# The second FFN product of a fused attention + FFN kernel in Strassen's form: seven block products in 128x256 matmuls in place of the plain product in 128x512 matmuls

## The chip, the cores and the metric

The kernel runs on one core of one Trainium2 chip. The metric is device time in microseconds (us), the median over runs. Differences of medians come with the ratio of the mean times: the mean time of one kernel's runs over the mean time of the other's runs in the same rounds, so it is not quite the ratio of the medians quoted beside it.

## The reference

Attention over 8 batches of 576 tokens gives 4608 tokens of 512 features, and an FFN follows.

```python
def _moe_ref(x, w_in, w_out):            # x [4608, 512], w_in [512, 2048], w_out [2048, 512]
    h = x @ w_in
    g = np.where(h > 0.0, h, np.exp(np.minimum(h, 0.0)) - 1.0)
    return (g @ w_out).astype(np.float32)      # the "second product"
```

The attention half (scores, softmax, product with v) is unchanged and only matters as work that shares the engines.

## The kernel before

The FFN works in tiles of tokens: two of 256 (tiles 0 and 1), then eight of 512 (tiles 2 to 9). For each tile and each of the 16 chunks of 128 hidden features there are four steps, on three engines:

```python
def F(t, i):      # TensorE: h = w_in[:, chunk].T @ x.T, four matmuls 128x512 into PSUM, where matmuls leave results ("hps", two banks)
def e(t, i):      # ScalarE: exp(h)
def r(t, i):      # VectorE: min(exp, 1) - 1, fp16
def g(t, i):      # VectorE: max(h, r) -> g, fp16 in SBUF; this also frees the hps bank
def G(t, tb_, qd):                 # TensorE: second product, 128 tokens, 4 of the 16 chunks
    for fc in range(4 * qd, 4 * qd + 4):
        nc.tensor.matmul(out=ob[t, tb_], lhsT=gts[t, fc][:, P * tb_:P * (tb_ + 1)], rhs=w_out16[:, fc, :],
                         start=(fc == 0), stop=(fc == NFC - 1))          # 128x512
def o(t, tb_):    # VectorE: PSUM -> SBUF, 128x512 f32
def s(t, tb_):    # DMA to out
```

From tile 3 on a plain loop orders the work. I call one pass over b a stage and one pass over i a slot. In the traces, from stage 3 on, r, g, evictions (o) start on VectorE in exactly the order in which the program emits them (256 of 256 in this kernel), and so do F and the second product's matmuls on TensorE (960). Weight loads overlap matmuls (in the page below both together are busy for more than the span).

```python
for b in range(3, NT // TT + 2):              # stages 3..10
    todo = ...                                # attention of the next batch, in 12 of 16 slots, for b < 8
    for i in range(NFC):                      # slots 0..15
        if b < len(tiles):                    # stages 3..9
            run(f"F.{b}.{i} e.{b}.{i} r.{b}.{i} g.{b}.{i}")
        run(f"G.{b - 1}.{i // 4}.{i % 4}")    # second product of the tile before
        if i % 4 == 3:
            run(f"o.{b - 1}.{i // 4} s.{b - 1}.{i // 4}")
        if i in todo: todo[i]()
```

So stages 3 to 7 carry attention too, stages 8 and 9 only FFN, and stage 10 only the second product of the last tile. Stage 2 is ordered by a hand-written list.

The softmax here doesn't subtract the row's maximum and nothing guards it: scores larger than these inputs give would overflow.

Of the kernel before, what the change touches and what calls it, by code (L numbers as in the profile page):

```python
# [8 lines left out]
FP32 = mybir.dt.float32  # L9
FP16 = mybir.dt.float16  # L10
BF16 = mybir.dt.bfloat16
AFT = mybir.ActivationFunctionType
ALU = mybir.AluOpType
# [4 lines left out]
def kernel(  # L18
# [11 lines left out]
    nc = tc.nc  # L30
    P = 128

    B, H, S, D = q.shape
# [3 lines left out]
    DM = H * D  # L37
# [18 lines left out]
    def layout(cuts):  # L56

        res, col = [], 0
        for qa, qe in zip(cuts, cuts[1:]):
# [10 lines left out]
    NFC = DF // P  # L70
    SCALE = float(1.0 / (D ** 0.5))
    tiles = [(0, CUT), (CUT, TT)] + [(t, t + TT) for t in range(TT, NT, TT)]
# [7 lines left out]
    konst = ctx.enter_context(tc.tile_pool(name="konst", bufs=1))  # L80
    stage = ctx.enter_context(tc.tile_pool(name="stage", bufs=2))
    attn = ctx.enter_context(tc.tile_pool(name="attn", bufs=2))
    xpool = ctx.enter_context(tc.tile_pool(name="xpool", bufs=4))
    melt = ctx.enter_context(tc.tile_pool(name="melt", bufs=3))
    gpool = ctx.enter_context(tc.tile_pool(name="gpool", bufs=2 * NFC + 2))
    psum = ctx.enter_context(tc.tile_pool(name="psum", bufs=2, space=bass.MemoryType.PSUM))
    ctx.enter_context(tc.manual_schedule(
        engines={ENG.PE, ENG.Activation, ENG.DVE, ENG.Pool, ENG.SP}))
# [3 lines left out]
            name=nc.get_next_instruction_name(),  # L92
# [6 lines left out]

    w_in16 = konst.tile([P, NCC, DF], FP16, name="w_in16")  # L100
    w_out16 = konst.tile([P, NFC, DM], FP16, name="w_out16")


    st = {}
# [29 lines left out]
    def load_wi(fa, fe):  # L134

        for g in range(2):
            for i in range(4):
                nc.gpsimd.dma_start(  # L138
                    out=w_in16[32 * i:32 * (i + 1), 2 * g:2 * g + 2, fa:fe], in_=wi_v[i, :, g, :, fa:fe])
# [5 lines left out]
    for b in range(B):  # L145
        (nc.sync if b % 2 == 0 else nc.scalar).dma_start(
            out=bk32[NB * b:NB * (b + 1), :, :],
            in_=beacon_k[b].rearrange("h n d -> n h d"))
# [7 lines left out]
    for t in qks:  # L156
# [12 lines left out]
        out=triu, in_=triu, compare_op=ALU.is_ge, fill=0.0, base=0,  # L169
# [13 lines left out]
    op = {}  # L183
# [76 lines left out]
    def S_(b, p, g):  # L260
        if g == 0:
            ets[b, p] = attn.tile([P, 2, ECOLS], FP16, tag="et", bufs=6, name="et")
        s = sc[b, p, g] = psum.tile([P, 2, 512], FP32, tag="S", name="sc")
        t = qkT[b, p]
        c0, c1 = GW * g, GW * (g + 1)
        for (j, qa, qe, col) in lays[b]:
            a, e = max(c0, col), min(c1, col + qe - qa)
            if a >= e:
                continue
            for h in range(2):  # L270
                nc.tensor.matmul(  # L271
                    out=s[:, h, a - c0:e - c0],
                    lhsT=t[D * h:D * (h + 1), 1, P * j:P * (j + 1)],
                    rhs=t[D * h:D * (h + 1), 0, NB + qa + a - col:NB + qa + e - col],
                    start=True, stop=True, skip_group_check=True,
                )
# [8 lines left out]
    @step  # L285
    def m(b, p, g):

        c0, c1 = GW * g, GW * (g + 1)
        for (j, qa, qe, col) in lays[b]:
            base = NB if j == 0 else 0  # L290
            e = min(qe, ilo[j] + P - base)
            a, e = max(qa, qa + c0 - col), min(e, qa + c1 - col)
            if a >= e:
                continue
            t0 = a - ilo[j] + base
            o = ets[b, p][0:kc[j], :, col + a - qa:col + e - qa]
            nc.vector.tensor_tensor(out=o, in0=o, in1=triu[0:kc[j], :, t0:t0 + e - a], op=ALU.mult)  # L297

    def quad(b, g, qa, qe, t, half, first):


        v16 = st[b][2]
        pcs = [(j, max(a, qa), min(e, qe), c + max(a, qa) - a) for (j, a, e, c) in lays[b]
               if max(a, qa) < min(e, qe)]
        for n, (j, a, e, c) in enumerate(pcs):
            for i in range(4):
                h, p = 4 * g + i, 2 * g + i // 2
                nc.tensor.matmul(  # L308
                    out=t[32 * i:32 * (i + 1), a - qa:e - qa],
                    lhsT=ones[0:kc[j], :] if half is None else v16[0:kc[j], j, h, 32 * half:32 * (half + 1)],  # L310
                    rhs=ets[b, p][0:kc[j], i % 2, c:c + e - a],
                    start=(first and n == 0), stop=(n == len(pcs) - 1), skip_group_check=True)
# [101 lines left out]
    op["R"] = R_  # L414


    hp, eb, rb, gts, ob = {}, {}, {}, {}, {}

    @step
    def F(t, i):  # L420
# [12 lines left out]
    def flat(y):  # L433
        return y.rearrange("c n w -> c (n w)")

    @step
    def e(t, i):
        eb[t, i] = melt.tile([P, 512], FP32, tag="e", name="e")
        nc.scalar.activation(out=eb[t, i], in_=flat(hp[t, i]), func=AFT.Exp, bias=0.0, scale=1.0)  # L439

    @step
# [4 lines left out]

    @step
    def g(t, i):
        w = tiles[t][1] - tiles[t][0]
        gt = gpool.tile([P, 512 // w, w], FP16, tag="g", name="gt")  # L450
        nc.vector.tensor_tensor(out=flat(gt), in0=flat(hp[t, i]), in1=rb[t, i], op=ALU.max)  # L451
        for n_ in range(512 // w):
            gts[t, i * (512 // w) + n_] = gt[:, n_, :]

    @step
    def G(t, tb_, qd):
        if qd == 0:
            ob[t, tb_] = psum.tile([P, DM], FP32, tag="ops", name="ops")
        for fc in range(4 * qd, 4 * qd + 4):
            nc.tensor.matmul(  # L460
                out=ob[t, tb_], lhsT=gts[t, fc][:, P * tb_:P * (tb_ + 1)], rhs=w_out16[:, fc, :],
                start=(fc == 0), stop=(fc == NFC - 1))

    @step
# [5 lines left out]
    @step  # L470
    def s(t, tb_):
        row = tiles[t][0] + tb_ * P
        nc.sync.dma_start(out=out[row:row + P, :], in_=ob[t, tb_])

    @step
    def wo(i):
# [12 lines left out]
    def run(names):  # L489
        for word in names.split():  # L490
            f, *args = word.split(".")
            op[f](*[a if a in "ABR" else int(a) for a in args])
# [26 lines left out]
    G.1.0.0 e.2.3 g.2.2 m.2.2.0 m.2.2.1 r.2.3 F.2.4 S.2.2.2 g.2.3 e.2.4 S.2.1.3 cb.3.2 x.2.2.2 r.2.4  # L519
    g.2.4 G.1.1.2 F.2.5 m.2.2.2 T.3.0 x.2.1.3 m.2.1.3 e.2.5 T.2.3 ck.3.0 ck.2.3 F.2.6 r.2.5 G.1.1.3  # L520
    g.2.5 e.2.6 S.2.2.3 S.2.3.0 F.2.8 o.1.1 cb.3.1 x.2.2.3 G.1.0.1 r.2.6 x.2.3.0 S.2.3.1 m.2.2.3
    L.2.0 e.2.8 x.2.3.1 W.2.0.0 g.2.6 W.2.0.1 m.2.3.0 s.0.0 r.2.8 g.2.8 s.0.1 m.2.3.1 F.2.7 n.2.0
    M.2.0.1 e.2.7 M.2.0.0 F.2.9 S.3.0.0 e.2.9 S.2.3.2 lv.3 G.1.0.2 r.2.7 g.2.7 x.3.0.0 x.2.3.2
    F.2.11 S.3.0.1 e.2.11 x.3.0.1 r.2.9 m.3.0.0 g.2.9 m.2.3.2 r.2.11 g.2.11 s.1.1 S.2.3.3 m.3.0.1
    F.2.10 x.2.3.3 G.1.0.3 e.2.10 S.3.0.2 m.2.3.3 o.1.0 x.3.0.2 S.3.0.3 F.2.12 r.2.10 m.3.0.2 g.2.10
    L.2.1 e.2.12 W.2.1.0 x.3.0.3 s.1.0 r.2.12 F.2.14 g.2.12 m.3.0.3 n.2.1 M.2.1.0 F.2.13 e.2.14
    T.3.1 W.2.1.1 e.2.13 r.2.14 R.2 ck.3.1 T.3.2 g.2.14 r.2.13 F.2.15 g.2.13 M.2.1.1 n.2.R M.2.R
    e.2.15 r.2.15 ck.3.2 g.2.15
    """)
# [1 line left out]
    def T_(b, p):  # L531
        if b < B:
            run(f"cb.{b}.{p} T.{b}.{p} ck.{b}.{p}")

    def SC(b, p, g0):
        if b < B:
            for g_ in (g0, g0 + 1):
                run(f"S.{b}.{p}.{g_} x.{b}.{p}.{g_} m.{b}.{p}.{g_}")

    def LW(b, g):  # L540
        run(f"L.{b}.{g} W.{b}.{g}.0 n.{b}.{g} M.{b}.{g}.0")

    def WR(b, g):
        run(f"W.{b}.{g}.1" + g * f" R.{b}" + f" M.{b}.{g}.1" + g * f" n.{b}.R M.{b}.R")

    SLOTS = [0, 1, 2, 4, 5, 6, 7, 8, 9, 11, 12, 13]
    for b in range(3, NT // TT + 2):
        todo = {}
        if b < B:
            todo = dict(zip(SLOTS, [  # L550
                lambda: SC(b, 1, 0), lambda: SC(b, 1, 2), lambda: (T_(b, 3), LW(b, 0)),
                lambda: SC(b, 2, 0), lambda: SC(b, 2, 2), lambda: (T_(b + 1, 0), WR(b, 0)),
                lambda: SC(b, 3, 0), lambda: SC(b, 3, 2), lambda: (T_(b + 1, 1), LW(b, 1)),
                lambda: SC(b + 1, 0, 0), lambda: SC(b + 1, 0, 2), lambda: (T_(b + 1, 2), WR(b, 1))]))
        for i in range(NFC):
            if b < len(tiles):
                run(f"F.{b}.{i} e.{b}.{i} r.{b}.{i} g.{b}.{i}")
            run(f"G.{b - 1}.{i // 4}.{i % 4}")
            if i % 4 == 3:
                run(f"o.{b - 1}.{i // 4} s.{b - 1}.{i // 4}")  # L560
            if i in todo:
                todo[i]()
            if i == 3 and b + 1 < B:
                run(f"lk.{b + 1} lv.{b + 1}")
# [28 lines left out]
```

## Time and profile before

| | before |
|---|---|
| time, median | 371.9 us |
| TensorE matmuls of the second product | 576 of 128x512 |
| one stage with attention (F of slot 0 to F of slot 0) | 40.1 to 40.3 us (stage 7, which has less: 37.0) |
| one FFN-only stage | 27.6 us |

The lines below are from the profile page of the kernel before: the busy time of the engines, then the shares of the chain that ended last, then groups of instructions. A group line reads: source line, engine, operation, output<-inputs, shapes, count | busy us, mean ns of one | idle us before it.

```profile
PE 361.5 (97%) x4427; PEld 182.1 (49%) x4427; DVE 251.9 (68%) x611; ACT 238.5 (64%) x351; POOL 68.4 (18%) x100
...
PE 88%; DMA 5%; POOL 4%; issue 1%; DVE 1%; ACT 1%; POOLq 0%
...
L460 PE MATMUL ops<-w_out_80,gt 128*128 128x512 f16 x576 | 145.3, 379 | 0.0
...
L451 DVE TENSOR_TENSOR gt<-hps,r 128x512 f16<-128x512 f32 x144 | 99.6, 692 | 5.8
...
L467 DVE COPY osb<-ops 128x512 f32<-128x512 f32 x36 | 24.6, 683 | 11.8 <-PE ops L460 11.8
```

TensorE (PE) is 97% busy and 88% of the chain. That alone doesn't prove that it runs at its rate, since matmul ends are modelled (a matmul shows 379 ns although they follow each other every 216 ns). The rate is read from starts, in the order-of-time view of TensorE (start us, duration us, what, count). The first two lines are from the 256-token tiles, the others are slots 3 and 4 of stage 6.

```profile
44.33 1.05 PE L429 MATMUL hps<-xT,w_in_79 128*128 128x256 f16 x8
45.21 1.03 PE L460 MATMUL ops<-w_out_80,gt 128*128 128x512 f16 x4
...
229.12 1.04 PE L429 MATMUL hps<-xT,w_in_79 128*128 128x512 f16 x4
229.99 1.03 PE L460 MATMUL ops<-w_out_80,gt 128*128 128x512 f16 x4
230.85 1.03 PE L429 MATMUL hps<-xT,w_in_79 128*128 128x512 f16 x4
231.72 1.03 PE L460 MATMUL ops<-w_out_80,gt 128*128 128x512 f16 x4
```

Four 128x512 matmuls take 229.99 - 229.12 = 0.87 us, 216 ns each; eight 128x256 take 45.21 - 44.33 = 0.88 us, 110 ns each. No line has an idle time in brackets: TensorE never waits here. VectorE at the same time (same kernel, order of time, brackets give idle time and what ended it):

```profile
230.55 0.76 DVE L378 TENSOR_TENSOR xT<-lt,rl 128x128 f16<-128x128 f32 x2 [1.88 <-ACT rl L344]
231.22 0.42 DVE L444 TENSOR_SCALAR r<-e 128x512 f16<-128x512 f32 x1
231.68 0.69 DVE L451 TENSOR_TENSOR gt<-hps,r 128x512 f16<-128x512 f32 x1
232.28 0.68 DVE L467 COPY osb<-ops 128x512 f32<-128x512 f32 x1
232.88 0.42 DVE L444 TENSOR_SCALAR r<-e 128x512 f16<-128x512 f32 x1
```

Here r, g and the eviction o of slot 3 stand one behind the other. Independent instructions start 0.60 us apart although they take 0.68 us.

### The profile page before, as it was taken

What the parts mean: (1) busy time and instruction counts of PE and PEld (TensorE: products, weight loads), DVE (VectorE), ACT (ScalarE), POOL (GpSimd) and SP (SyncE); (2) the same over time, 40 slices, a digit from 0 to 9 for tenths busy, and PEclk for the clock granted to TensorE, in tenths of its full rate; (3) what the DMA queues carried; (4) which work ended last, traced back from release to release, by engine and by line L of the source; (5) the groups of instructions that cost most, each with busy time, mean ns of one, the idle gap of its engine ahead of it and who ended that gap; (6) DMA issues with size and microseconds to landing.
All of it is one profiled execution on the core that took longest, in us unless ns stands there. A gap on an engine that the chain in (4) does not pass through costs nothing.

```text
span 371.1 us, 10275 instructions
## 1 busy us (share of the span) xinstructions
PE 361.5 (97%) x4427; PEld 182.1 (49%) x4427; DVE 251.9 (68%) x611; ACT 238.5 (64%) x351; POOL 68.4 (18%) x100
## 2 busy tenths in 40 slices
PE   8989989999999999999999999999999999999995
PEld 3567655444554454444444454445444544444442
DVE  2448876777777678667767676766767777777731
ACT  2999977788787766777577757776677333333300
POOL 8876530510330014000510050000000000000000
PEclk9999999999999999999999999999999999999999
DMA  8999999945296019900973065000000001001012
GB/s 122 170 167 195 180 196 199 94 60 100 43 90 123 31 32 94 156 32 28 97 104 82 29 42 58 30 30 30 30 30 31 30 28 58 29 28 58 28 59 84
DMA packets 61101, 28.84 MB, mean 78 GB/s; under 512 B 41088, under 2 KB 55424, under 8 KB 61056
## 3 DMA queue, kind: packets, MB, share of 16 engines
q0 software_dynamic: 54720, 18.49, 45.1%
q1 hardware_dynamic: 5760, 9.57, 7.0%
q8 instruction: 34, 0.56, 0.6%
q10 hardware_dynamic: 576, 0.13, 0.2%
q14 instruction: 11, 0.09, 0.1%
HBM read 37.22 MB, written 9.44 MB: 126 GB/s over the span
## 4 chain that ended last, share of the span: by engine, by line
PE 88%; DMA 5%; POOL 4%; issue 1%; DVE 1%; ACT 1%; POOLq 0%
PE hps L429 34%; PE ops L460 33%; PE sc L271 7%; PE lt L308 5%; DMA kst<-in_k_dram 5%; PE tp L229 4%; PE ut L308 4%; POOL v_124 L126 1%; DMA w_in_79<-in_moe_w_in_dram 1%; POOL qst L113 1%; POOL kst L113 1%; DVE xT L378 1%; PE ub L308 0%; POOL w_in_79 L138 0%; ACT rl L344 0%
## 5 line engine op out<-in xcount | busy, mean ns | idle before, releaser
L429 PE MATMUL hps<-xT,w_in_79 128*128 128x512 f16 (+1 forms) x640 | 147.6, 359 | 0.1
L460 PE MATMUL ops<-w_out_80,gt 128*128 128x512 f16 x576 | 145.3, 379 | 0.0
L439 ACT ACTIVATE e<-hps 128x512 f32<-128x512 f32 x144 | 86.4, 600 | 63.5 <-PE hps L429 63.4
L281 ACT ACTIVATE et<-sc 128x832 f16<-128x832 f32 x128 | 104.2, 872 | 16.3 <-PE sc L271 16.2
L451 DVE TENSOR_TENSOR gt<-hps,r 128x512 f16<-128x512 f32 x144 | 99.6, 692 | 5.8
L460 PEld LDWEIGHTS <-gt 128*128 128x128 f16 x576 | 55.8, 98 | 66.3 <-issue 0.9
L444 DVE TENSOR_SCALAR r<-e 128x512 f16<-128x512 f32 x144 | 63.7, 442 | 31.5 <-ACT e L439 29.7
L429 PEld LDWEIGHTS <-w_in_79 128*128 128x128 f16 x640 | 56.2, 98 | 56.2 <-issue 5.7
L297 DVE TENSOR_TENSOR et<-et,triu 128x256 f16<-128x256 f16 (+2 forms) x164 | 40.7, 270 | 25.8 <-ACT et L281 25.5
L467 DVE COPY osb<-ops 128x512 f32<-128x512 f32 x36 | 24.6, 683 | 11.8 <-PE ops L460 11.8
L378 DVE TENSOR_TENSOR xT<-lt,rl 128x448 f16<-128x448 f32 (+6 forms) x28 | 10.6, 419 | 21.0 <-ACT rl L344 21.0
L229 PEld LDWEIGHTS <-qst 96*64 96x64 bf16 x384 | 10.2, 109 | 10.7 <-issue 10.3
L378 DVE TENSOR_TENSOR xT<-ut,rl 128x448 f16<-128x448 f32 (+6 forms) x28 | 10.6, 419 | 6.8 <-PE ut L308 5.3
L198 PE MATMUL w_151<-zero 64*128 64x512 bf16 (+1 forms) x39 | 13.0, 454 | 1.3 <-DVE zero L150 1.3
L229 PE MATMUL tp<-identb,kst 96*64 96x96 bf16 x348 | 12.3, 206 | 1.3 <-DMA kst<-in_k_dram 1.3
L113 POOL DMA_DIRECT2D qst<-in_q_dram x12 | 8.8, 729 | 25.2 <-PE tp L229 21.1
L229 PE MATMUL tp<-identb,qst 96*64 96x96 bf16 x348 | 12.9, 209 | 0.4 <-ACT et L281 0.4
L344 ACT ACTIVATE rl<-rl 128x512 f32<-128x512 f32 (+2 forms) x23 | 12.4, 538 | 0.7
L308 PEld LDWEIGHTS <-ones 128*32 128x32 f16 (+1 forms) x624 | 10.4, 95 | 5.1 <-issue 1.8
L341 ACT ACTIVATE rl<-lt 128x512 f32<-128x512 f32 (+1 forms) x15 | 9.1, 605 | 5.9 <-PE lt L308 5.9
L308 PE MATMUL lt<-et,ones 128*32 128x512 f16 (+7 forms) x320 | 11.9, 279 | 0.0
L229 PEld LDWEIGHTS <-kst 96*64 96x64 bf16 x384 | 10.5, 110 | 1.4 <-DMA kst<-in_k_dram 1.4
(94 smaller groups left out, 234.3 us busy)
## 6 DMA issues: line engine op xcount, KB each, us to landing
out_dram<-osb SPq DMA_DIRECT2D x36, 256.0 KB, 2.0
qst<-in_q_dram POOLq DMA_DIRECT2D x6, 576.0 KB, 6.6
kst<-in_k_dram POOLq DMA_DIRECT2D x6, 576.0 KB, 9.8
w_in_79<-in_moe_w_in_dram POOLq DMA_DIRECT2D x16, 128.0 KB, 6.3
w_out_80<-in_moe_w_out_dram POOLq DMA_DIRECT2D x4, 512.0 KB, 10.9
qst<-in_q_dram POOLq DMA_DIRECT2D x4, 144.0 KB, 4.3
kst<-in_k_dram POOLq DMA_DIRECT2D x4, 144.0 KB, 4.4
qst<-in_q_dram POOLq DMA_DIRECT2D x2, 288.0 KB, 7.0
```

Source lines behind the costliest of these rows:

```text
L229: nc.tensor.transpose(out=dst[D * h:D * (h + 1), PR * r:PR * (r + 1)], in_=src[:, 2 * p + h, r, :], identity=identb[0:PR, 0:PR],)
L271: nc.tensor.matmul(out=s[:, h, a - c0:e - c0], lhsT=t[D * h:D * (h + 1), 1, P * j:P * (j + 1)], rhs=t[D * h:D * (h + 1), 0, NB + qa + a - ...
L281: nc.scalar.activation(out=ets[b, p][:, :, GW * g:GW * (g + 1)], in_=sc[b, p, g][:, :, 0:GW], func=AFT.Exp, bias=0.0, scale=SCALE)
L297: nc.vector.tensor_tensor(out=o, in0=o, in1=triu[0:kc[j], :, t0:t0 + e - a], op=ALU.mult)
L308: nc.tensor.matmul(out=t[32 * i:32 * (i + 1), a - qa:e - qa], lhsT=ones[0:kc[j], :] if half is None else v16[0:kc[j], j, h, 32 * half:32 * ...
L378: nc.vector.tensor_tensor(out=x_tile(k)[:, cc, tok - TT * k:to - TT * k], in0=u[:, o:o + to - tok], in1=r[:, o:o + to - tok], op=ALU.mult)
L429: nc.tensor.matmul(out=h[:, n_, :], lhsT=w_in16[:, cc, P * fc:P * (fc + 1)], rhs=xt[k][:, cc, a - TT * k:e - TT * k], start=(cc == 0), sto ...
L439: nc.scalar.activation(out=eb[t, i], in_=flat(hp[t, i]), func=AFT.Exp, bias=0.0, scale=1.0)
L444: nc.vector.tensor_scalar(out=rb[t, i], in0=eb[t, i], scalar1=1.0, scalar2=1.0, op0=ALU.min, op1=ALU.subtract)
L451: nc.vector.tensor_tensor(out=flat(gt), in0=flat(hp[t, i]), in1=rb[t, i], op=ALU.max)
L460: nc.tensor.matmul(out=ob[t, tb_], lhsT=gts[t, fc][:, P * tb_:P * (tb_ + 1)], rhs=w_out16[:, fc, :], start=(fc == 0), stop=(fc == NFC - 1))
L467: nc.vector.tensor_copy(out=osb, in_=ob[t, tb_])
```

## The change

The intent is to save one in eight of the matmul columns. Per tile g is cut into 2x2 blocks A (256 tokens x 1024 hidden features, even and odd chunks), w_out into 2x2 blocks B (1024 x 256). The Winograd form of Strassen's scheme needs seven block products:

- sums of g per tile ("Z"): S3 = A11 - A21, then in place S1 = A21 + A22 (over A21), S2 = S1 - A11 (over A11), S4 = A12 - S2 (over A12), each in two halves h = 0, 1 by hidden features;
- sums of w_out once ("wt"): T1 = B12 - B11, T2 = B22 - T1, T4 = B21 - T2, and B22 - B12 over B12;
- seven phases of 16 matmuls of 128x256 in two PSUM banks X and Y: X = A11 B11; Y = A12 B21; X += S2 T2; Y = S1 T1; X += S3 (B22 - B12); Y += S4 B22; X += A22 T4. Between them the banks are copied by ScalarE (three times, and once at the end) or added to such a copy by VectorE (three times).

So 64 matmuls of 128x512 a tile become 112 of 128x256, that is 7/8 of the columns. The core of the diff (cut):

```diff
-    xpool = ... bufs=4 ;  gpool = ... bufs=2 * NFC + 2
+    xpool = ... bufs=3 ;  gpool = ... bufs=4              # one tile for half of a tile's g
+    PH = [(0, (0, 0), B11, True), (1, (1, 0), B21, True), (0, (0, 0), T2, False), (1, (0, 1), T1, True),
+          (0, None, B12, False), (1, (1, 0), B22, False), (0, (1, 1), T4, False)]
+    def Q(t, ph, qd):                     # half a phase: 8 matmuls 128x256
+        n_, src, wt_, first = PH[ph]
+        for c in range(NPR):
+            lw = s3[:, c] if src is None else A(t, c // HP, *src)[:, c % HP]
+            nc.tensor.matmul(out=xy[t, n_][:, qd, :], lhsT=lw[:, P * qd:P * (qd + 1)], rhs=wt_[:, c, :], ...)
+    def J(t, ph):                         # after phases 0, 2, 3, 6 a ScalarE copy, after 1, 4, 5 a VectorE add
+    # stage 2's list: wt.1.0 wt.1.1 wt.2.0 wt.2.1 wt.4.0 wt.4.1 put between the steps
+    HS = [0, 1, 2, 3, 4, 5, 7, 8, 9, 10, 11, 12, 14, 15]      # slots with half a phase
+    SUMS = {0: [(-1, 1, 1)], 2: [(-1, 2, 0)], 3: [(-1, 2, 1)], 5: [(-1, 4, 0)], 7: [(-1, 4, 1)],
+            11: [(0, 3, 0)], 13: [(0, 1, 0)], 15: [(0, 3, 1)]}  # slot: (tile, which sum, half)
     for b in range(3, NT // TT + 2):
+        if b == 3:
+            run("wt.3.0 wt.3.1 Z.2.3.0 Z.2.1.0 Z.2.3.1")
         for i in range(NFC):
             F e r g
-            run(f"G.{b - 1}.{i // 4}.{i % 4}")
-            if i % 4 == 3: o s
+            if i in HS:
+                n_ = HS.index(i)
+                run(f"Q.{b - 1}.{n_ // 2}.{n_ % 2}")
+                if n_ % 2: run(f"J.{b - 1}.{n_ // 2}")
+            for dt_, n_, h_ in SUMS.get(i, []): run(f"Z.{b + dt_}.{n_}.{h_}")
```

Phase 2 (X += S2 T2) starts in slot 4, and the second half of S2 is emitted in slot 3, after that slot's g and after J of phase 1. The cut leaves out that e has two buffers in place of three.

More of the change, by code (lines that the diff above doesn't have):

```diff
@@ L82 @@
     attn = ctx.enter_context(tc.tile_pool(name="attn", bufs=2))
-    xpool = ctx.enter_context(tc.tile_pool(name="xpool", bufs=4))
+    xpool = ctx.enter_context(tc.tile_pool(name="xpool", bufs=3))
     melt = ctx.enter_context(tc.tile_pool(name="melt", bufs=3))
-    gpool = ctx.enter_context(tc.tile_pool(name="gpool", bufs=2 * NFC + 2))
+    gpool = ctx.enter_context(tc.tile_pool(name="gpool", bufs=4))
     psum = ctx.enter_context(tc.tile_pool(name="psum", bufs=2, space=bass.MemoryType.PSUM))
@@ L101 @@
     w_out16 = konst.tile([P, NFC, DM], FP16, name="w_out16")
+    NPR = NFC // 2
+    HM = DM // 2
+    w4 = w_out16.rearrange("p (c j) (s m) -> p c j s m", j=2, s=2)
+    B11, B12, B21, B22 = (w4[:, :, j, s_, :] for j in range(2) for s_ in range(2))
+    T1, T2, T4 = (konst.tile([P, NPR, HM], FP16, name=f"wt{i}") for i in (1, 2, 4))
+    s3 = konst.tile([P, NPR, HM], FP16, name="s3")
     st = {}
@@ L414 @@
     op["R"] = R_
-    hp, eb, rb, gts, ob = {}, {}, {}, {}, {}
+    hp, eb, rb, gh, ob = {}, {}, {}, {}, {}
+    UN = NFC // 2
     @step
@@ L437, in e @@
     def e(t, i):
-        eb[t, i] = melt.tile([P, 512], FP32, tag="e", name="e")
+        eb[t, i] = melt.tile([P, 512], FP32, tag="e", bufs=2, name="e")
         nc.scalar.activation(out=eb[t, i], in_=flat(hp[t, i]), func=AFT.Exp, bias=0.0, scale=1.0)
@@ L448, in g @@
     def g(t, i):
-        w = tiles[t][1] - tiles[t][0]
-        gt = gpool.tile([P, 512 // w, w], FP16, tag="g", name="gt")
-        nc.vector.tensor_tensor(out=flat(gt), in0=flat(hp[t, i]), in1=rb[t, i], op=ALU.max)
-        for n_ in range(512 // w):
-            gts[t, i * (512 // w) + n_] = gt[:, n_, :]
+        k = t, i // UN
+        if k not in gh:
+            gh[k] = gpool.tile([P, UN, 512], FP16, tag="g", name="gt")
+        nc.vector.tensor_tensor(out=gh[k][:, i % UN, :], in0=flat(hp[t, i]), in1=rb[t, i], op=ALU.max)
     @step
@@ L458, in G @@
             ob[t, tb_] = psum.tile([P, DM], FP32, tag="ops", name="ops")
+        gt = gh[t, 0].rearrange("p u (n w) -> p (u n) w", n=2)
         for fc in range(4 * qd, 4 * qd + 4):
             nc.tensor.matmul(
-                out=ob[t, tb_], lhsT=gts[t, fc][:, P * tb_:P * (tb_ + 1)], rhs=w_out16[:, fc, :],
+                out=ob[t, tb_], lhsT=gt[:, fc, P * tb_:P * (tb_ + 1)], rhs=w_out16[:, fc, :],
                 start=(fc == 0), stop=(fc == NFC - 1))
@@ L473, in s, with A, sub, wt @@
         nc.sync.dma_start(out=out[row:row + P, :], in_=ob[t, tb_])
+    def A(t, h_, j, i):
+        v_ = gh[t, h_].rearrange("p (c j) (i w) -> p c j i w", j=2, i=2)
+        return v_[:, :, j, i, :]
+    def sub(o_, a_, b_, op_=ALU.subtract):
+        nc.vector.tensor_tensor(out=o_, in0=a_, in1=b_, op=op_)
+    HP = NPR // 2
+    @step
+    def wt(n, h_):
+        c = slice(HP * h_, HP * (h_ + 1))
+        if n == 1:
+            sub(T1[:, c], B12[:, c], B11[:, c])
+        elif n == 2:
+            sub(T2[:, c], B22[:, c], T1[:, c])
+        elif n == 3:
+            sub(B12[:, c], B22[:, c], B12[:, c])
+        else:
+            sub(T4[:, c], B21[:, c], T2[:, c])
@@ new lines, in Z @@
+    @step
+    def Z(t, n, h_):
+        c = slice(HP * h_, HP * (h_ + 1))
+        if n == 3:
+            sub(s3[:, c], A(t, h_, 0, 0), A(t, h_, 0, 1))
+        elif n == 1:
+            sub(A(t, h_, 0, 1), A(t, h_, 0, 1), A(t, h_, 1, 1), ALU.add)
+        elif n == 2:
+            sub(A(t, h_, 0, 0), A(t, h_, 0, 1), A(t, h_, 0, 0))
+        else:
+            sub(A(t, h_, 1, 0), A(t, h_, 1, 0), A(t, h_, 0, 0))
+    xy, sm = {}, {}
+    PH = [(0, (0, 0), B11, True), (1, (1, 0), B21, True), (0, (0, 0), T2, False), (1, (0, 1), T1, True),
+          (0, None, B12, False), (1, (1, 0), B22, False), (0, (1, 1), T4, False)]
@@ new lines, in Q @@
+    @step
+    def Q(t, ph, qd):
+        if (t, 0) not in xy:
+            for n_ in (0, 1) if t % 2 == 0 else (1, 0):
+                xy[t, n_] = psum.tile([P, 2, HM], FP32, tag="ops", name="ops")
+        n_, src, wt_, first = PH[ph]
+        for c in range(NPR):
+            lw = s3[:, c] if src is None else A(t, c // HP, *src)[:, c % HP]
+            nc.tensor.matmul(
+                out=xy[t, n_][:, qd, :], lhsT=lw[:, P * qd:P * (qd + 1)], rhs=wt_[:, c, :],
+                start=(first and qd == 0 and c == 0), stop=(c == NPR - 1), skip_group_check=True)
@@ new lines, in J @@
+    @step
+    def J(t, ph):
+        if ph in (0, 2, 3):
+            sm[t, ph] = melt.tile([P, 2, HM], FP32, tag="sm", name="sm")
+            nc.scalar.copy(out=sm[t, ph], in_=xy[t, PH[ph][0]])
+            return
+        osb = melt.tile([P, 2, HM], FP32, tag="osb", name="osb")
+        src = xy[t, PH[ph][0]]
+        if ph == 6:
+            nc.scalar.copy(out=osb, in_=src)
+        else:
+            nc.vector.tensor_tensor(out=osb, in0=src, in1=sm[t, {1: 0, 4: 3, 5: 2}[ph]], op=ALU.add)
+        i, m_ = {1: (0, 0), 4: (1, 1), 5: (0, 1), 6: (1, 0)}[ph]
+        row = tiles[t][0] + 256 * i
+        nc.sync.dma_start(
+            out=out[row:row + 256, HM * m_:HM * (m_ + 1)].rearrange("(q p) m -> p q m", p=P), in_=osb)
@@ L521 @@
     g.2.5 e.2.6 S.2.2.3 S.2.3.0 F.2.8 o.1.1 cb.3.1 x.2.2.3 G.1.0.1 r.2.6 x.2.3.0 S.2.3.1 m.2.2.3
-    L.2.0 e.2.8 x.2.3.1 W.2.0.0 g.2.6 W.2.0.1 m.2.3.0 s.0.0 r.2.8 g.2.8 s.0.1 m.2.3.1 F.2.7 n.2.0
-    M.2.0.1 e.2.7 M.2.0.0 F.2.9 S.3.0.0 e.2.9 S.2.3.2 lv.3 G.1.0.2 r.2.7 g.2.7 x.3.0.0 x.2.3.2
-    F.2.11 S.3.0.1 e.2.11 x.3.0.1 r.2.9 m.3.0.0 g.2.9 m.2.3.2 r.2.11 g.2.11 s.1.1 S.2.3.3 m.3.0.1
-    F.2.10 x.2.3.3 G.1.0.3 e.2.10 S.3.0.2 m.2.3.3 o.1.0 x.3.0.2 S.3.0.3 F.2.12 r.2.10 m.3.0.2 g.2.10
-    L.2.1 e.2.12 W.2.1.0 x.3.0.3 s.1.0 r.2.12 F.2.14 g.2.12 m.3.0.3 n.2.1 M.2.1.0 F.2.13 e.2.14
+    L.2.0 e.2.8 x.2.3.1 W.2.0.0 g.2.6 W.2.0.1 m.2.3.0 s.0.0 r.2.8 g.2.8 s.0.1 m.2.3.1 F.2.7 wt.1.0 n.2.0
+    M.2.0.1 e.2.7 M.2.0.0 F.2.9 wt.1.1 S.3.0.0 e.2.9 S.2.3.2 lv.3 G.1.0.2 r.2.7 g.2.7 x.3.0.0 x.2.3.2
+    F.2.11 wt.2.0 S.3.0.1 e.2.11 x.3.0.1 r.2.9 m.3.0.0 g.2.9 m.2.3.2 r.2.11 g.2.11 s.1.1 S.2.3.3 m.3.0.1
+    F.2.10 wt.2.1 x.2.3.3 G.1.0.3 e.2.10 S.3.0.2 m.2.3.3 o.1.0 x.3.0.2 S.3.0.3 F.2.12 wt.4.0 r.2.10 m.3.0.2 g.2.10
+    L.2.1 e.2.12 W.2.1.0 x.3.0.3 s.1.0 r.2.12 F.2.14 wt.4.1 g.2.12 m.3.0.3 n.2.1 M.2.1.0 F.2.13 e.2.14
     T.3.1 W.2.1.1 e.2.13 r.2.14 R.2 ck.3.1 T.3.2 g.2.14 r.2.13 F.2.15 g.2.13 M.2.1.1 n.2.R M.2.R
@@ L557 @@
                 run(f"F.{b}.{i} e.{b}.{i} r.{b}.{i} g.{b}.{i}")
-            run(f"G.{b - 1}.{i // 4}.{i % 4}")
-            if i % 4 == 3:
-                run(f"o.{b - 1}.{i // 4} s.{b - 1}.{i // 4}")
+            if i in HS:
+                n_ = HS.index(i)
+                run(f"Q.{b - 1}.{n_ // 2}.{n_ % 2}")
+                if n_ % 2:
+                    run(f"J.{b - 1}.{n_ // 2}")
+            for dt_, n_, h_ in SUMS.get(i, []):
+                if b + dt_ < len(tiles):
+                    run(f"Z.{b + dt_}.{n_}.{h_}")
             if i in todo:
```

## The prediction

> **What bounds it now.** TensorE. The stretches view shows PE busy 10.00 of every 10 us from 100 us to 360 us at a granted clock of 1.00. In order of time, four F products and four second-product matmuls (both 128x512) alternate in blocks of 0.864 us: 216 ns each, no holes. VectorE is 68-78% busy, ScalarE 35-75%.
>
> **Removed and added on TensorE.** Per tile of 512 tokens, 64 matmuls of 128x512 become 112 of 128x256. The trace has 128x256 already: in the first two tiles eight F matmuls, each with its own weights, take 0.88 us, 110 ns each. So the 98 ns weight load stays hidden; this agrees with the Trainium skill, "TensorE: Matmul & The Clock Gate", section "Back-to-back issue gap" (N/2.4 + 2.5 ns warm). 64 x 216 = 13.8 us becomes 112 x 110 = 12.3 us: 1.5 us a tile, 12 us for eight tiles (3.2%). All of it is on the chain that ended last.
>
> **Added on VectorE.** Eight sums a tile of 1024 fp16 elements per partition. The mask products give the rate: 128x256 288 ns, 128x224 271 ns, so 0.53 ns per element and some 150 ns fixed. That is two elements a cycle, as the skill's "VectorE: DVE Perf Modes" says for 16-bit tensor_tensor. Estimate 0.69 us, 0.63 us start to start; 5 us a tile. Four evictions of 0.68 us become three adds of about 0.69. ScalarE gets four 0.6 us copies. In the FFN-only stages VectorE then works about 24 of 26 us: nearly full, not the bound by itself.
>
> **Where the gain goes.** The order within the stage. Phase 2 of the new product (slot 4) needs the second half of its sum, which stands behind g of slot 3 and behind the phase-1 eviction on VectorE. In the trace of an attention stage F of slot 3 starts at 229.12, g of that slot ends at 232.37, and the eviction starts at 232.28; the sum would then end at about 233.6. The PE wants it at 231.72 + 0.44 = 232.16: a stall of 1.5 us. By the same reckoning 1.1 us in the FFN-only stages and the last. So 5 x 1.5 + 3 x 1.1 = 11 us, nearly all of the gain.
>
> Further: start of stage 3, five sums (3.2 us) ahead of r, F of slot 2 waits for g of slot 0: about 2 us. Six weight sums where VectorE is already over 80% busy (84-100 us): about 1 us. Slots 6 and 13 have no second product, so in FFN-only stages two F come close together, while F to end of g takes 2.85 us and there are two hps banks: about 1 us. Last stage: 0.5 us for g of slot 15; last output in 1 KB rows 0.3 us. Sum: -12 + 11 + 5 = +4; I take some overlap off.
>
> **Predicted 375 us, 8 in 10 between 366 and 380.** Faster by over 2%: 0.08; within 2%: 0.80; slower by over 2%: 0.12.
>
> **What would show it.** 128x256 matmuls spaced 110 ns in the new product (right), over 120 ns (weight load exposed, wrong). PE idle or stretched matmuls once a stage, four matmuls into phase 2, released by the VectorE sum, 1-1.5 us each. Sums of 0.65-0.75 us; over 1.1 us means one element a cycle, and VectorE becomes the bound of the FFN-only stages. Stages 3 to 7 about as long as before (37-38 us); FFN-only stages 27-28 us against 27.7.
>
> **What would make it wrong.** Faster: the wait at phase 2 is shorter than reckoned, because the PE comes late to slot 4 for other reasons; then some 365. Slower: slow sums or coarse dependencies (a whole half of g counted as one), so that VectorE and PE wait in turn; then over 380.

## The result

The changed kernel takes 377.5 us (376.7 to 377.6, four runs) against 371.9 us: ratio 1.0144, 95% interval 1.013 to 1.0159. It is correct. TensorE has some 11% less to do in the second product of a 512-token tile, and the kernel is 1.4% slower.

The profile page after, the same parts:

```profile
PE 352.2 (94%) x4811; PEld 219.8 (58%) x4811; DVE 286.5 (76%) x675; ACT 253.7 (67%) x383; POOL 68.5 (18%) x100
...
PE 57%; DVE 20%; ACT 10%; issue 5%; POOL 3%; DMA 3%; ACTq 0%; DVEq 0%; POOLq 0%
...
L531 PE MATMUL ops<-wt,gt 128*128 128x256 f16 x384 | 50.5, 273 | 9.3 <-DVE gt L489 9.3
...
L489 DVE TENSOR_TENSOR gt<-gt 128x1024 f16<-128x1024 f16 x48 | 32.5, 682 | 0.1
...
L547 DVE TENSOR_TENSOR osb<-ops,sm 128x512 f32<-128x512 f32 x24 | 16.4, 682 | 5.6 <-issue 4.6
```

VectorE now has 20% of the chain, where it had 1%. A new idle time stands in front of the product's matmuls, ended by the sums of line 489. The waits view of the changed kernel (who waited for whom: total us, times, longest us) gives their number, eight, one per tile; the third line is a second wait, of F on g, that was not there before.

```profile
PEld L531 <- DVE gt L489: 11.5, 8, 1.6
...
PE ops L531 <- DVE gt L489: 9.3, 8, 1.3
...
PE hps L436 <- DVE gt L459: 3.5, 6, 1.7
```

Slots 3 and 4 of stage 6 after, TensorE in order of time, and below them slots 5 to 7 of stage 8, where slot 6 has no second product:

```profile
232.72 1.04 PE L436 MATMUL hps<-xT,w_in 128*128 128x512 f16 x4
233.60 1.04 PE L531 MATMUL ops<-w_out,gt 128*128 128x256 f16 x8
234.47 1.03 PE L436 MATMUL hps<-xT,w_in 128*128 128x512 f16 x4
235.33 0.60 PE L531 MATMUL ops<-wt,gt 128*128 128x256 f16 x4
237.22 0.61 PE L531 MATMUL ops<-wt,gt 128*128 128x256 f16 x4 [1.29 <-DVE gt L489]
237.77 0.53 PE L277 MATMUL sc<-qk 64*128 64x416 bf16 x6
...
313.30 1.04 PE L531 MATMUL ops<-wt,gt 128*128 128x256 f16 x8
314.17 2.19 PE L436 MATMUL hps<-xT,w_in 128*128 128x512 f16 x8
316.19 1.04 PE L531 MATMUL ops<-wt,gt 128*128 128x256 f16 x8
```

The product's eight matmuls take 234.47 - 233.60 = 0.87 us: the narrow form runs at 109 ns. But the second four of phase 2 start 1.89 us after the first four, where 0.44 us would do: 1.45 us are lost. Below, eight F matmuls take 316.19 - 314.17 = 2.02 us in place of 1.73: 0.29 us are lost where two F stand together. VectorE in the same slots of stage 6:

```profile
234.83 0.42 DVE L451 TENSOR_SCALAR r<-e 128x512 f16<-128x512 f32 x1
235.28 0.69 DVE L459 TENSOR_TENSOR gt<-hps,r 128x512 f16<-128x512 f32 x1
235.89 0.68 DVE L547 TENSOR_TENSOR osb<-ops,sm 128x512 f32<-128x512 f32 x1
236.49 0.68 DVE L489 TENSOR_TENSOR gt<-gt 128x1024 f16<-128x1024 f16 x1
```

The sum ends at 236.49 + 0.68 = 237.17, and at 237.22, 0.05 us later, TensorE goes on. It stood behind r, g and the eviction, as the queue before had shown that it would. The longest wait of F on g is at slot 2 of stage 3, behind the five sums at the start of that stage:

```profile
107.56 0.81 PE L436 MATMUL hps<-xT,w_in 128*128 128x512 f16 x3 [1.66 <-DVE gt L459]
```

From the starts of F in the traces, stage by stage (us from F of slot 0 to F of slot 0 of the next; the last row is from the last F matmul to the end of TensorE's work). The last column is the experiment e1 below.

| stage | before | after | e1 |
|---|---|---|---|
| 2 | 32.70 | 34.61 | 34.21 |
| 3 | 40.06 | 42.39 | 40.92 |
| 4, 5, 6 | 40.26, 40.26, 40.06 | 40.38, 40.36, 40.36 | 38.90 each |
| 7 | 37.03 | 37.94 | 36.48 |
| 8 | 27.63 | 27.70 | 26.63 |
| last F to end of TensorE | 15.06 | 14.66 | 13.48 |

In stages 4 to 6 and 8 the gain and the loss cancel to within 0.1 to 0.3 us. Stages 2, 3 and 7 lose on top.

### The profile page after: what moved, and what is told of

Its sections match the earlier page's. It is cut to its first block, busy times and chain, and to the rows that moved or that the text cites. A ratio compares the mean times of both kernels' runs of the same rounds, so it can differ in the third digit from the quotient of the medians.

```text
span 375.9 us, 11164 instructions
## 1 busy us (share of the span) xinstructions
PE 352.2 (94%) x4811; PEld 219.8 (58%) x4811; DVE 286.5 (76%) x675; ACT 253.7 (67%) x383; POOL 68.5 (18%) x100
## 4 chain that ended last, share of the span: by engine, by line
PE 57%; DVE 20%; ACT 10%; issue 5%; POOL 3%; DMA 3%; ACTq 0%; DVEq 0%; POOLq 0%
PE hps L436 22%; PE ops L531 18%; DVE gt L459 5%; PE lt L314 5%; PE sc L277 5%; ACT et L287 4%; DVE r L451 4%; PE ops L468 3%; DVE xT L384 3%; PE tp L235 3%; DVE osb L547 3%; DVE gt L489 2%; DMA kst<-in_k_dram 2%; PE ut L314 2%; ACT rl L350 2%
## 5 line engine op out<-in xcount | busy, mean ns | idle before, releaser
L436 PE MATMUL hps<-xT,w_in 128*128 128x512 f16 (+1 forms) x640 | 147.7, 359 | 4.4 <-DVE gt L459 3.5
L436 PEld LDWEIGHTS <-w_in 128*128 128x128 f16 x640 | 56.3, 97 | 51.7 <-issue 12.0
L531 PE MATMUL ops<-wt,gt 128*128 128x256 f16 x384 | 50.5, 273 | 9.3 <-DVE gt L489 9.3
L531 PE MATMUL ops<-w_out,gt 128*128 128x256 f16 x384 | 49.1, 273 | 0.0
L277 PE MATMUL sc<-qk 64*128 64x208 bf16 (+9 forms) x528 | 36.6, 249 | 2.0 <-ACT et L287 1.1
L256 ACT COPY qk<-tp 128x1152 bf16<-128x1152 bf16 x29 | 32.5, 1134 | 3.9 <-PE tp L235 3.8
L132 POOL DMA_DIRECT2D v<-in_v_dram x40 | 34.2, 885 | 4.6 <-DMA kst<-in_k_dram 2.6
L489 DVE TENSOR_TENSOR gt<-gt 128x1024 f16<-128x1024 f16 x48 | 32.5, 682 | 0.1
L277 PEld LDWEIGHTS <-qk 64*128 64x128 bf16 x528 | 19.0, 94 | 22.6 <-issue 16.0
L314 PEld LDWEIGHTS <-v 128*32 128x32 f16 x1248 | 21.2, 94 | 9.2 <-issue 2.5
```

The costliest lines, as they stand in the source:

```text
L132: nc.gpsimd.dma_start(out=st[b][2][r0:r0 + n, j, :, :], in_=v[b, :, ilo[j]:ilo[j] + n, :].rearrange("h s d -> s h d"),)
L256: nc.scalar.copy(out=t[:, :, NB:SK].rearrange("c i (p r) -> c i p r", r=R), in_=tps[b, p][:, :, 0:S].rearrange("c i (r p) -> c i p r", r=R))
L277: nc.tensor.matmul(out=s[:, h, a - c0:e - c0], lhsT=t[D * h:D * (h + 1), 1, P * j:P * (j + 1)], rhs=t[D * h:D * (h + 1), 0, NB + qa + a - ...
L314: nc.tensor.matmul(out=t[32 * i:32 * (i + 1), a - qa:e - qa], lhsT=ones[0:kc[j], :] if half is None else v16[0:kc[j], j, h, 32 * half:32 * ...
L436: nc.tensor.matmul(out=h[:, n_, :], lhsT=w_in16[:, cc, P * fc:P * (fc + 1)], rhs=xt[k][:, cc, a - TT * k:e - TT * k], start=(cc == 0), sto ...
L489: nc.vector.tensor_tensor(out=o_, in0=a_, in1=b_, op=op_)
```

## The experiments

Three theories were put to the test. Theory A: the narrower matmuls do save what they should, and the gain is lost in a few waits that come from the order of VectorE's queue. Theory B: VectorE has too much work (35 us more than before), so any order would lose it. Theory C: the 128x256 form is dearer than half of the 128x512 form. All experiments but e3 gave correct results.

### e1: the second half of the sum one slot earlier

```diff
-    SUMS = {0: [(-1, 1, 1)], 2: [(-1, 2, 0)], 3: [(-1, 2, 1)], 5: ...
+    SUMS = {0: [(-1, 1, 1)], 2: [(-1, 2, 0), (-1, 2, 1)], 5: ...
```

> The second half of the sum for phase 2 moves from slot 3 (behind that slot's g and the eviction of phase 1) to slot 2; same work on every engine. Theory A (the gain of the narrower matmuls is lost in a wait that the order on VectorE makes): the eight waits at phase 2 go, 5 x 1.48 + 2 x 1.09 + 1.2 us = 10.8 us, so about 366.7 us, between 365.5 and 368.5, and faster than the kernel before. Theory B (VectorE has too much work, the wait would only move elsewhere): within 1 us of 377.5. Theory C (matmuls of 128x256 cost more than half of 128x512): within 1 us of 377.5.

Measured: 367.2 us (366.3 to 367.7), ratio to the kernel before 0.9871 (0.9852 to 0.989). The change of one entry of a table is worth 10.3 us, and the kernel is now faster than the kernel before by 1.3%. Slots 3 and 4 of stage 6 on TensorE, in order of time:

```profile
227.73 1.04 PE L436 MATMUL hps<-xT,w_in 128*128 128x512 f16 x4
228.60 1.04 PE L531 MATMUL ops<-w_out,gt 128*128 128x256 f16 x8
229.48 1.03 PE L436 MATMUL hps<-xT,w_in 128*128 128x512 f16 x4
230.34 1.04 PE L531 MATMUL ops<-wt,gt 128*128 128x256 f16 x8
231.31 0.53 PE L277 MATMUL sc<-qk 64*128 64x416 bf16 x6
```

VectorE from slot 2 on, in order of time, in the same kernel:

```profile
227.31 1.28 DVE L489 TENSOR_TENSOR gt<-gt 128x1024 f16<-128x1024 f16 x2
228.51 0.17 DVE L245 COPY qk<-bkT 128x16 bf16<-128x16 bf16 x1
229.16 0.76 DVE L384 TENSOR_TENSOR xT<-lt,rl 128x128 f16<-128x128 f32 x2 [0.48 <-ACT rl L350]
```

All eight matmuls of phase 2 stand in one line without a wait. Both sums now stand in a gap that VectorE had anyway, while it waited for ScalarE: the gap was 1.88 us before the change, 1.08 us in the changed kernel, which has one of the two sums there, and is 0.48 us here. So the moved sum costs nothing. Slot by slot, stages 3 to 7 are 1.46 to 1.48 us shorter between the F of slot 4 and that of slot 5, and nowhere else by more than 0.1 us, the FFN-only stages 1.07, the last one 1.18: 5 x 1.47 + 2 x 1.07 + 1.18 = 10.7 us. Theories B and C fall as the main cause.

### e2: in slot 3, the sum ahead of the eviction

```diff
-                if n_ % 2: run(f"J.{b - 1}.{n_ // 2}")
+                if n_ % 2 and i != 3: run(f"J.{b - 1}.{n_ // 2}")
             for dt_, n_, h_ in SUMS.get(i, []): ...
+            if i == 3: run(f"J.{b - 1}.1")
```

> In slot 3 the sum goes ahead of the eviction of phase 1, nothing else moves. Theory A: each of the eight waits is shorter by one eviction, 0.60 us start to start, so 4.8 us less than 377.5: 372.7, between 371.7 and 373.7. Theories B and C: within 1 us of 377.5.

Measured: 372.4 us (372.2 to 372.6), ratio 1.0014 to the kernel before (0.9999 to 1.0029). That is 5.1 us less than the 377.5 of the changed kernel. The wait of stage 6, TensorE in order of time:

```profile
233.71 0.60 PE L531 MATMUL ops<-wt,gt 128*128 128x256 f16 x4
235.00 0.61 PE L531 MATMUL ops<-wt,gt 128*128 128x256 f16 x4 [0.69 <-DVE gt L489]
```

From the first to the second four it is 1.29 us now against 1.89: exactly one instruction of VectorE, 0.60 us, less, and so in each of stages 3 to 9. In the last stage, which has no r and g, the whole wait of 1.18 us goes, which is why the gain is a little over 4.8 us. The size of the wait follows the place in the queue. In this trace too r, g, evictions and sums start in exactly the order of the program.

### e3: no sums (wrong result)

```diff
     def sub(o_, a_, b_, op_=ALU.subtract):
+        return
-    PH = [..., (0, (0, 0), T2, False), (1, (0, 1), T1, True), (0, None, B12, False), ..., (0, (1, 1), T4, False)]
+    PH = [..., (0, (0, 0), B22, False), (1, (0, 1), B12, True), (0, (0, 1), B12, False), ..., (0, (1, 1), B21, False)]
```

> Wrong result on purpose: no sums of g and of w_out at all, the seven products take raw blocks; all 112 matmuls of 128x256 a tile and all evictions stay. Theory A: the whole gain on TensorE shows, 12 us less about 1.5 us for the slots in which two F products stand together: 361 to 362 us. Theory B: the same, since VectorE is relieved of 36 us of work. Theory C: no gain, 370 or more.

Measured: 362.1 us (361.3 to 362.4), ratio 0.9734 (0.9719 to 0.9748). This is the ceiling of the change in this order of TensorE: 9.8 us less than before. Of the 5.1 us between e1 and e3, 4.5 lie in stage 2 (34.21 against 32.53), stage 3 (40.92 against 38.67) and stage 7 (36.48 against 35.90), so in the weight sums, in the start of the scheme and in a wait of F on g at the ends of stages 3 and 7 (0.54 and 0.58 us), not in the steady stages, which are equal within 0.14 us (38.90 against 38.76 to 38.88).

### e4: the sums of the third kind done twice

```diff
-            11: [(0, 3, 0)], 13: [(0, 1, 0)], 15: [(0, 3, 1)]}
+            11: [(0, 3, 0), (0, 3, 0)], 13: [(0, 1, 0)], 15: [(0, 3, 1), (0, 3, 1)]}
```

> The two sums of the third kind are done twice (same result), in slots 11 and 15, where no wait of TensorE on a sum was seen: 7 x 1.25 us = 8.8 us more work on VectorE. Theory A: hardly any change, 377.5 to 379. Theory B: most of the added work shows, 384 to 387. Theory C: no change.

Measured: 380.9 us (380.1 to 384.4; the slowest is the profiled run, which lost 3.7 us before stage 2, where nothing was changed, in part to a late load of k), ratio 1.0234 to the kernel before. So 3.4 us more than the changed kernel for 8.8 us more work: more than A, less than B had expected. In the trace stages 4 to 6 are 0.3 us longer, stages 7 to 9 by 0.7 to 0.8. The place is a wait that I had overlooked, F on g. Slots 13 and 14 of stage 8, on TensorE:

```profile
331.29 1.03 PE L436 MATMUL hps<-xT,w_in 128*128 128x512 f16 x4
333.10 1.02 PE L436 MATMUL hps<-xT,w_in 128*128 128x512 f16 x4 [0.79 <-DVE gt L459]
```

Slot 13 has no second product, so F of slot 14 comes right behind F of slot 13 and needs the hps bank that g of slot 12 frees. The doubled sum of slot 11 delays that g, and F of slot 14 comes 0.65 us later in each FFN-only stage: there VectorE has no slack in slots 11 to 13. In stages 4 to 7 the added time stands elsewhere, in front of F of slot 0 of the next stage (0.24 to 0.72 us), behind the doubled sum of slot 15.

### e9: the same amount of extra sums, in other slots

The expectation of e4 had failed, so the same 14 extra sums were put elsewhere, on the changed kernel.

```diff
+    spare = konst.tile([P, NPR // 2, HM], FP16, name="spare")
...
+            if i in (4, 9) and b < len(tiles):
+                sub(spare, A(b - 1, 0, 1, 1), A(b - 1, 0, 0, 1))
```

> As e4, 14 sums of the same size more on VectorE than in the changed kernel (8.8 us), but into a spare tile and in slots 4 and 9, where VectorE had gaps in front of r, instead of slots 11 and 15. Theory A (what counts is in front of which wait a sum stands): at most 0.7 us more than 377.5, so 377 to 378.2. Theory B (the amount of work counts): as in e4 again, about 380.9.

Measured: 377.1 us (376.7 to 377.4), ratio 1.0137 (1.0111 to 1.0163), the same as the changed kernel's 1.0144. So 14 sums cost 3.4 us in slots 11 and 15 and nothing in slots 4 and 9. (Slot 4 is where TensorE itself waits in this kernel; whether sums there are free in e1's order was not run.) The waits view shows it. First e4:

```profile
PEld L531 <- DVE gt L489: 11.6, 9, 1.6
...
PE hps L436 <- DVE gt L459: 6.8, 11, 1.6
```

The same view of e9, where the two added lines of code shift the line numbers by one:

```profile
PEld L532 <- DVE gt L490: 11.5, 8, 1.6
...
PE hps L437 <- DVE gt L460: 3.7, 7, 1.6
```

The wait of F on g is 6.8 us in e4 and 3.7 us in e9, against 3.5 us in the changed kernel. At this size, it is not the amount of work on VectorE that counts but what each instruction stands in front of.

### e8: the narrow matmul by itself

The kernel before, with each 128x512 matmul of the second product cut in two.

```diff
-            nc.tensor.matmul(out=ob[t, tb_], lhsT=..., rhs=w_out16[:, fc, :], ...)
+            for m_ in range(2):
+                nc.tensor.matmul(out=ob[t, tb_][:, 256 * m_:256 * (m_ + 1)], lhsT=...,
+                                 rhs=w_out16[:, fc, 256 * m_:256 * (m_ + 1)], ...)
```

> The kernel before, with each 128x512 matmul of the second product cut into two of 128x256 with the same weights: no saving, only the cost of the narrow form by itself. At 110 ns against half of 216 ns it is 4 ns a pair, 576 pairs: 2 us, about 374 us (Theory A). Theory C (the narrow form is dear, the weight load is exposed): 378 us or more.

Measured: 374.3 us (374.0 to 374.6), ratio 1.0052 (1.0034 to 1.0071): 2.1 us more, so theory C falls. Not all of the 2.1 us can be laid to the narrow form. By starts in the traces, narrow matmuls follow each other every 109.2 ns on average and wide ones every 216.0 ns: 2.5 ns a pair, 1% more per column, 1.4 us for 576 pairs, and stages 3 and 5 to 9 are 0.14 to 0.16 us longer each. Stage 4 is 1.85 us longer, 1.75 us of it in one slot: a matmul of attention, which the edit doesn't touch, came late there (last line below). Why it did, and whether it did so in the runs without a profile, is not known. TensorE in an FFN-only stage, then that matmul:

```profile
302.59 1.03 PE L429 MATMUL hps<-xT,w_in 128*128 128x512 f16 x4
303.45 1.04 PE L461 MATMUL ops<-w_out,gt 128*128 128x256 f16 x8
304.33 1.03 PE L429 MATMUL hps<-xT,w_in 128*128 128x512 f16 x4
...
177.55 0.21 PE L308 MATMUL ut<-et,v 80*32 80x64 f16 x2 [1.55 <-issue]
```

Four wide ones take 0.86 us, eight narrow ones 0.88 us.

### e5 and e6: the start sums moved into gaps

The weight sums T1 and T2 go to two gaps of VectorE earlier in stage 2, the first sums of g to a gap at the end of stage 2, and the other weight sums to slots 4, 6, 8 and 10 of stage 3. e5 has this on top of e1, e6 has it alone.

```diff
-    stage 2: ... F.2.7 wt.1.0 ... F.2.9 wt.1.1 ... F.2.11 wt.2.0 ... F.2.10 wt.2.1 ... F.2.12 wt.4.0 ... F.2.14 wt.4.1
+    stage 2: ... F.2.8 wt.1.0 wt.1.1 o.1.1 ... F.2.7 wt.2.0 wt.2.1 n.2.0 ... g.2.13 Z.2.3.0 Z.2.1.0 M.2.1.1 ...
-        if b == 3: run("wt.3.0 wt.3.1 Z.2.3.0 Z.2.1.0 Z.2.3.1")
+        if b == 3: run("Z.2.3.1")
+    WS = {4: "wt.3.0", 6: "wt.3.1", 8: "wt.4.0", 10: "wt.4.1"}     # slots of stage 3
```

> On top of e1_both_in_slot2: the block sums of w_out and the first sums of g move to gaps of VectorE in stage 2 and to later slots of stage 3; only one sum stays ahead of r at the start of stage 3. Theory A: the one wait of 1.7 us at slot 2 of stage 3 nearly goes, and 1 to 1.5 us of the lengthened stage 2: 364 to 365 us, from 367.2. Theory B (VectorE has too much work there wherever it stands): within 1 us of 367.2.

> The same move of the start sums without the move to slot 2. Theory A: the two waits add up, so as much less than 377.5 as e5 is less than 367.2: 374 to 375 us, with the eight waits at phase 2 unchanged. Theory B: within 1 us of 377.5.

Measured: e5 364.3 us (363.9 to 364.6), ratio 0.9786 to the kernel before (0.9769 to 0.9802), 2.9 us less than e1. e6 374.35 us (374.3 to 374.8), ratio 1.0059 (1.0043 to 1.0075), 3.2 us less than the changed kernel. The two moves add up, so the two losses are separate. In the traces stage 2 falls from 34.21 us in e1 to 32.48 us in e5, 1.7 us and somewhat more than expected; stage 3 only from 40.92 to 40.25, because of the 1.73 us at its slot 2 some 0.75 us came back at slot 1 and 0.3 us at slot 7.

### e7: an even spread in the FFN-only stages

```diff
+            if b in (8, 9):                       # seven matmuls to a slot, in place of eight or none
+                for m_ in range(7 * i, 7 * i + 7):
+                    Q(b - 1, m_ // 16, m_ // 8 % 2, [m_ % 8])
+                    if m_ % 16 == 15: run(f"J.{b - 1}.{m_ // 16}")
-            if i in HS: ...
+            elif i in HS: ...
```

The sums of these two stages move along: the second half of S2 to slot 3 again (phase 2 begins later there), the last three to slots 12, 14 and 15. The spread and this move were not run apart.

> On top of e5: in the two FFN-only stages the 112 matmuls are spread seven to a slot, so that no two F products stand together. Theory A: the 0.3 us lost at slots 7 and 14 of these stages goes: 4 x 0.3 = 1.2 us less than e5, about 363 us, nearly the 362.1 us of the kernel without sums. Theory B: these stages have VectorE at 24 us of work in 26 us, so up to 1 us less only.

Measured: 362.6 us (362.5 to 363.9), ratio 0.9748 (0.9727 to 0.977), 1.7 us less than e5 by the medians; in the traces stage 8 falls from 26.63 to 26.04 us and the rest to the last F of stage 9 from 25.54 to 25.06, together 1.1 us: each slot is 0.11 us shorter, and slots 6 and 13, which now have matmuls of the product too, 0.46 us longer. This version beats both kernels: 2.5% faster than before, and 0.9748 / 1.0144 = 0.961 of the time of the change as given. One stretch of its FFN-only stages (busy us of TensorE, weight loads, VectorE, ScalarE and GpSimd, each with its count, then granted clock, DMA share and GB/s):

```profile
320.00:330.00 10.00, 10.00 (x68) 6.55 (x67) 9.51 (x19) 4.37 (x8) 0.00 (x0) 1.00 0.16 52
```

VectorE is 95% busy here, more than in the changed kernel (7.5 to 9.1 us of 10), and TensorE has no wait. This too speaks against theory B.

## Why the prediction was right or wrong

The prediction was 375 us with 366 to 380 as its range; 377.5 us came out, inside it, and "within 2%" was the likeliest class and the true one. The two largest terms, the gain of 12 us and the wait of 11 us, were right in mechanism and size. That the number came within 2.5 us is in part luck: of the small terms one was too small, one was not there, and two places were overlooked. Point by point:

- **Gain on TensorE, 12 us.** Right. 109 ns in the product (0.87 us for eight), and e8 shows 2.5 ns a pair where 4 ns were reckoned. The formula that the Trainium skill ("TensorE: Matmul & The Clock Gate", section "Back-to-back issue gap") gives for an isolated matmul, N/2.4 + 2.5 ns, holds for both widths in the streams here: 215.8 and 109.2 ns against 216.0 and 109.2 ns measured.
- **Sums of 0.69 us, 0.63 us apart.** Right: 682 ns, 0.60 us apart. VectorE takes two fp16 elements a cycle in such a sum, as the skill says of 16-bit operands ("VectorE: DVE Perf Modes", section "Side-by-side: where the cycles go for N=2048 bf16"). The traces agree: a sum of 1024 fp16 elements takes 682 ns, about as long as an eviction of 512 fp32 elements (683 ns).
- **The wait at phase 2, 1.5 us in attention stages and 1.1 in the others, 11 us in all.** Right in place, cause and size: 1.47, 1.07 and 1.18 us, 10.7 us. e1 takes it away, e2 shortens it by just one instruction in stages 3 to 9.
- **Start of stage 3, about 2 us; slots 6 and 13, about 1 us.** Right: 1.73 us at slot 2; 0.29 us at each of four places in the FFN-only stages. In e5 the first wait goes, though 0.75 and 0.3 us come back elsewhere; in e7 the second goes.
- **Six weight sums in stage 2, about 1 us.** Too small: stage 2 became 1.9 us longer (1.4 to 2.0 us among the traces of e1, e2, e4, e9 and the changed kernel, which have the same stage 2), and e5 got 1.7 us of it back.
- **0.5 us for g of slot 15 in the last stage.** Not there: the first 32 matmuls of that stage follow without a break, in 361.58 - 358.09 = 3.49 us, 109 ns each. The last output was 0.2 us later in this trace (0.0 to 0.2 us in those of the experiments), not 0.3.
- **Overlooked: the ends of stages 3, 6 and 7.** F of slot 0 of the next stage waited for g there (0.55, 0.23 and 0.6 us; e3, without sums, doesn't have it).
- **Overlooked: slot 6 of stages 3 to 6.** Without sums (e3) it is only 0.66 us shorter than before, where slot 13 is 0.77 to 0.86 us shorter: 0.1 to 0.2 us lost in each.
- **Stages 3 to 7 "about as long as before (37-38 us)".** As long as before holds for stages 4 to 6 (0.1 to 0.3 us longer), but the figure is wrong: before, only stage 7 took 37 us, the others 40.1 to 40.3.
- **"I take some overlap off": the step that was off.** The terms of the prediction summed to +4, and 375 is +3. Nothing overlaps in what was tested: e5 and e6 show that the waits at phase 2 and the start sums add up. As measured, -12 + 10.7 + 1.7 + 1.2 + 1.9 + 0.6 + 0.2 = +4.3, against +5.6 between the medians (and +4.8 between the spans of the two profiled executions, of which the changed one happened to be 0.9 us faster in the part ahead of stage 2). The ends of stages 3 and 6 (0.8 us) and slot 6 of stages 3 to 6 (0.7 us) bring it to +5.8. All these are read from single traces, so the agreement is good to a few tenths of a us and no better.

What remains open: in stage 3 some 1.6 us (e7 40.26 us against e3 38.67) are still lost in the best version, 0.74 at slot 1, 0.31 at slot 7 and 0.54 at its end, and 0.6 us at the end of stage 7. They were not pursued.

## What to carry to other kernels

A change that takes work off the bounding engine and adds work to a second one is judged by what each added instruction stands in front of in the second engine's queue, not by that engine's busy share: 14 extra sums of one size cost 3.4 us in one pair of slots and nothing in another, and in one stretch VectorE ran at 95% without holding TensorE up. Before giving such a change up, write down for each new operand when its consumer wants it and what stands ahead of its producer, using times of the old trace; here one table entry turned 1.4% slower into 1.3% faster. Gaps in which the second engine waits for a third were the place for the new work here.

## What the Trainium skill lacked or had wrong

- "TensorE: Matmul & The Clock Gate", section "Back-to-back issue gap", says that at N = 512 a sustained stream of weight loads and matmuls runs at about 131 ns per matmul and that N/2.4 + 2.5 over-counts there. Here such a stream, each matmul with its own weights (loads of 98 ns), ran at 216 ns for N = 512 and 109 ns for N = 256, what that formula gives, with no weight load exposed; 131 ns was not seen. For N = 256 in a stream the section has no figure.
- No page on VectorE gives a start-to-start time for two instructions of which the second writes the same tile as the first. In e4 two such sums of 0.68 us took 1.41 us together, so they started 0.73 us apart, where independent instructions started 0.60 us apart.
- No page has it that a second engine can cost 10.3 us at 76% busy over the span (the changed kernel against e1), or be 95% busy over a stretch without holding TensorE up (e7), according to the order of its queue.
